# A start-up stage re-ordered: dummies, transposes, weights and first tiles moved in a fused attention and gated feed-forward kernel

## The chip, the cores and the metric

The kernel runs on one core of one Trainium2 chip. The metric is device time in microseconds of one execution; the kernel before was run three times, and its time is the median. A profile is one more execution, recorded by the hardware profiler. The engines are named as in the profile: PE is TensorE's matrix multiply, PEld its weight load, DVE is VectorE, ACT is ScalarE, POOL is GpSimd, SP is SyncE, which issues DMAs only. Each engine works through its own queue in the order in which the program was written, and waits at semaphores for others.

## The reference

Two layers follow each other: an attention with 32 learned inducing points over each batch (`mab` is used twice), and a feed-forward with a sigmoid gate.

```python
def mab(q, kv):                       # m = 32, C = 128, scale = 1/sqrt(C)
    s = scale * (q @ kv.transpose(0, 2, 1))
    s = s - s.max(-1, keepdims=True)
    a = np.exp(s)
    a /= a.sum(-1, keepdims=True) + 1e-09
    return a @ kv
h = mab(I, x)                         # x: (4, 12416, 128), I: (4, 32, 128)
y = mab(x, h)                         # (4, 12416, 128)
gate = 1.0 / (1.0 + np.exp(-(y @ w_gate)))   # w_gate, w_val: (128, 1536)
out = (gate * (y @ w_val)) @ w_out           # w_out: (1536, 128)
```

So there are two stages to each batch. Stage 1 reduces the whole of x to h, 32 rows of 128. Stage 2 gives each token 32 weights on those rows, and the feed-forward follows. The second `a @ kv` is never formed: h is multiplied into w_gate and w_val first (`hw`), so that a token's 32 weights are turned directly into its 1536 gate and value numbers.

## The kernel before

A batch's 12416 tokens are 97 chunks of 128: six groups of 16 (`groups[0]` to `groups[5]`) and one chunk alone (`groups[6]`). The core works on batch 0's stage 1 first. This is the prologue, some 34 us, with nothing else to run beside it; in the loop that follows, stage 1 and the weights of later groups and batches run in slots beside the feed-forward.

**The prologue's stage 1.** x of batch 0 is loaded by groups, in the order of `arrival`: 0, 6, 1, 2, 3, 4, 5. The last group is loaded as 12 chunks and then 4. For each group TensorE transposes the chunks (`x_turn`, line 637), VectorE and ScalarE copy the result to `xT` (639, 641), TensorE computes the scores (`s1_score_pe`, 210), VectorE their maximum, negated (`s1_max`, 222), ScalarE the exponentials (`s1_exp`, 235), TensorE turns these (`s1_turn_pe`, 248), VectorE copies them out (`s1_turn_copy`, 254), and TensorE sums x with them as weights (`s1_sum_pe`, 270). Each group has a maximum of its own. The first four groups to arrive are joined early by GpSimd (`pool_part`, 676 and 680, into `hpart[0]`). The last three, `sa` = 3, `sb` = 4 and `sc` = 5, are joined at the end: `ml` is the least negated maximum of each row (714), L719 and L720 turn `ml` and lay the group maxima `nml` into one tile `low_ps`, VectorE takes the least over the four row groups (`top`, 723), L733 adds it to all rows, and ScalarE's exponential of that is the factor of each group (`wl`, 743). The sums are scaled by `wl` and added by matmuls with e32 (`h_add`, 762); the denominators are summed into `e32l` and through L768 inverted (330). Their product is `hT` (335).

**Last group.** Its first eight chunks go through `x_turn`; the last eight through a tile `xt` of two banks, at line 695. ScalarE copies the first four (697), VectorE the last four (701).

**Dummies.** `keep_on(n, tag)` issues n matmuls of 512 columns on constant data (line 103), whose results nobody reads. Their operand `idle` is the last four chunks of `xT[0]`, which are overwritten only when the last group's last four chunks are copied in; after that a dummy reads those.

**From hT to the loop.** TensorE computes the scores of the first 16 chunks of stage 2 (443), four of them first, and `hw` (341, copied by ScalarE at 351). The first four chunks (block 0) take a short way: maximum, exponential, sum and inverse on VectorE and ScalarE, then sixteen transposes (808) into `a2T`, and two copies by VectorE into `a2first` (812).

**The loop.** A block is four chunks, 512 tokens. Its 12 slices of 128 columns (`j`) are worked on in eight steps of two or one slices. In a step TensorE fills the gate (`g`) and the value (`v`) banks (`hidden_mm`, 853), ScalarE takes the tanh of the gate (873), VectorE forms the product (886), and TensorE projects it through `wo16` into `acc` (917). `hidden_mm` takes rows 0 or 32 of `hw` for a gate and 64 or 96 for a value, by `j % 2`. The gate of step t + 2 is filled behind the value of step t. `blocks[i]` lists the pieces of a block as (batch, first chunk, chunks); before, block 0 has one piece, and only the very first gate fill is cut in two halves, by `cut`.

PSUM tiles with the same tag (g1, v1, g2, v2, m, acc) share their banks: a tile waits until the one before it is read.

## Time and profile before

| | us |
|---|---|
| median of three runs | 726.5 |
| lowest and highest | 725.6 and 726.69 |
| the profiled execution | 728.19 |
| its span | 726.4 |
| first tanh of the loop starts | 33.97 |

The profiled execution is 1.8 us longer than its span, which is what lies around it, and 1.7 us above the median. Rows of the timeline read: start, length, engine, line, operation, out<-in, shape and count, and in brackets the idle time of the engine just before and what ended it. In the chain of waits each row is a piece of the path that ended last: start, length, what. Lengths of a group of several instructions reach from the first's start to the last's end.

### The profile page before, as it was taken

Reading aid. Unit: us, or ns where it says so; the run is one execution under the profiler, and the core shown is the slowest. Engines: PE = TensorE matmul, PEld = TensorE weight load, DVE = VectorE, ACT = ScalarE, POOL = GpSimd, SP = SyncE. Lnnn points to the kernel's source line nnn. Section 1 sums busy time; section 2 is a strip of 40 time slices with the busy share of each in tenths; the row PEclk is TensorE's granted clock in tenths of the full one; section 3 lists DMA queues with packets and bytes.
Section 4 is the critical chain, followed back from the end, with each engine's and each line's share of the span. In section 5 each row is a group of like instructions: output and inputs, shape, how many; then the busy total and the mean of one; then the engine's idle time right before and its main releaser. Section 6 shows DMA issues by size and latency. Waiting matters only on the chain.

```text
span 726.4 us, 21535 instructions
## 1 busy us (share of the span) xinstructions
PE 647.0 (89%) x8461; PEld 391.5 (54%) x8461; DVE 704.7 (97%) x870; ACT 673.9 (93%) x1007; POOL 419.6 (58%) x702
## 2 busy tenths in 40 slices
PE   6888898999998988999988989999999899898887
PEld 3555555555555555555555555555555555555555
DVE  4699999999999999999999999999999999999998
ACT  4499999999999999999999999999999999999996
POOL 4373845788754548488657265387865665636200
PEclk9999999999999999999999999999999999999999
DMA  9789654152649262325177531320322123121211
GB/s 171 133 164 194 130 107 102 59 109 70 83 115 172 69 138 69 80 74 120 51 111 168 104 84 39 80 75 30 76 59 74 45 60 62 53 63 45 61 45 46
DMA packets 116726, 65.21 MB, mean 90 GB/s; under 512 B 99824, under 2 KB 101008, under 8 KB 116624
## 3 DMA queue, kind: packets, MB, share of 16 engines
q1 hardware_dynamic: 111936, 49.81, 30.7%
q0 software_dynamic: 4416, 13.90, 10.7%
q8 instruction: 66, 1.08, 0.7%
q14 instruction: 36, 0.29, 0.2%
q10 hardware_dynamic: 272, 0.13, 0.1%
HBM read 27.80 MB, written 25.43 MB: 73 GB/s over the span
## 4 chain that ended last, share of the span: by engine, by line
DVE 50%; issue 20%; PE 15%; ACT 10%; DMA 3%; DVEq 1%; POOL 0%; SPq 0%; ACTq 0%; POOLq 0%
DVE u L886 48%; ACT t L873 9%; PE acc_ps L917 7%; PE v_ps L853 6%; DMA xn<-in_x_dram 2%; DVE nm L222 1%; DVEq L886 1%; DMA xT<-xn 1%; PE hp_ps L270 1%; PE g_ps L853 1%; PE s_ps L210 0%; POOL xn L81 0%; PE xt_ps L637 0%; ACT a1T L235 0%; ACT hwt L351 0%
## 5 line engine op out<-in xcount | busy, mean ns | idle before, releaser
L886 DVE SCALAR_TENSOR_TENSOR u<-t,v_ps 128x512 f16<-128x512 f16 (+1 forms) x778 | 675.6, 945 | 1.8 <-PE g_ps L853 0.9
L873 ACT ACTIVATE t<-g_ps 128x512 f16<-128x512 f32 (+1 forms) x777 | 594.0, 818 | 28.8 <-ACT t L873 16.9
L853 PE MATMUL v_ps<-a2r,hwt 32*128 32x512 f16 (+1 forms) x1188 | 293.3, 371 | 65.7 <-DVE u L886 65.0
L917 PE MATMUL acc_ps<-wo,u 128*128 128x128 f16 x4656 | 327.4, 220 | 0.0
L917 PEld LDWEIGHTS <-u 128*128 128x128 f16 x4656 | 261.0, 98 | 87.9 <-issue 86.9
L853 PE MATMUL g_ps<-a2r,hwt 32*128 32x512 f16 (+1 forms) x1188 | 296.5, 377 | 0.0
L853 PEld LDWEIGHTS <-hwt 32*128 32x128 f16 x2402 | 90.7, 91 | 197.8 <-issue 152.8
L512 POOL TENSOR_TENSOR sum<-e 128x256 f32<-128x256 f16 (+1 forms) x23 | 15.4, 672 | 144.1 <-ACT e L504 142.6
L558 POOL TENSOR_TENSOR a2n<-e,rs 128x2048 f16<-128x2048 f16 (+3 forms) x25 | 86.8, 3474 | 5.3 <-DVE rs L530 2.4
L536 POOL TENSOR_TENSOR near<-sme,minus 128x16 f32<-128x16 f32 (+1 forms) x22 | 65.2, 2963 | 1.8
L935 ACT ACTIVATE o<-acc_ps 128x512 f32<-128x512 f32 x96 | 58.3, 607 | 0.0
L491 POOL TENSOR_SCALAR rise<-rise 128x256 f32<-128x256 f32 (+6 forms) x110 | 51.0, 464 | 9.7
L490 POOL TENSOR_TENSOR rise<-sc 128x256 f32<-128x256 f32 (+1 forms) x22 | 16.2, 738 | 38.8 <-ACT sc L480 38.5
L492 POOL TENSOR_TENSOR top<-top,rise 128x128 f32<-128x128 f32 (+3 forms) x88 | 28.3, 321 | 7.3
L512 POOL TENSOR_TENSOR sum<-sum 128x128 f32<-128x128 f32 (+3 forms) x92 | 28.3, 307 | 7.2
L490 POOL TENSOR_TENSOR rise<-top 128x128 f32<-128x128 f32 (+3 forms) x88 | 27.2, 309 | 6.9
L495 POOL TENSOR_TENSOR sc<-sc,top 128x512 f32<-128x512 f32 (+1 forms) x22 | 23.8, 1084 | 1.7
L443 PEld LDWEIGHTS <-xT 128*128 128x128 f16 x388 | 13.2, 96 | 11.7 <-issue 11.7
L443 PE MATMUL s_ps<-hT,xT 128*128 128x32 f16 x388 | 18.1, 178 | 0.3 <-DVE hT L335 0.3
L235 ACT ACTIVATE a1T<-s_ps,nm 128x512 f16<-128x512 f32 (+1 forms) x25 | 15.7, 629 | 2.0 <-DVE nm L222 2.0
L492 POOL TENSOR_TENSOR top<-sc,rise 128x256 f32<-128x256 f32 (+1 forms) x22 | 16.3, 739 | 1.8
L81 POOL DMA_DIRECT2D xn<-in_x_dram x25 | 14.7, 597 | 4.4 <-DMA xn<-in_x_dram 3.6
(131 smaller groups left out, 237.0 us busy)
## 6 DMA issues: line engine op xcount, KB each, us to landing
out_dram<-o SPq DMA_DIRECT2D x96, 256.0 KB, 2.3
xn<-in_x_dram POOLq DMA_DIRECT2D x19, 512.0 KB, 8.2
xn<-in_x_dram POOLq DMA_DIRECT2D x4, 544.0 KB, 5.8
a2r<-a2n SPq DMA_TRANSPOSE x29, 4.5
xn<-in_x_dram POOLq DMA_DIRECT2D x1, 384.0 KB, 14.9
wg<-in_moe_w_gate_dram POOLq DMA_DIRECT2D x1, 384.0 KB, 16.3
wv<-in_moe_w_val_dram POOLq DMA_DIRECT2D x1, 384.0 KB, 16.6
wo<-in_moe_w_out_dram POOLq DMA_DIRECT2D x1, 384.0 KB, 16.0
```

The source lines that it names most:

```text
L443: nc.tensor.matmul(s2[:, j, :], xT[b][:, c + j, :], hT16[b][:], start=(j == 0), stop=whole and j == j1 - 1, skip_group_check=True,)
L490: nc.gpsimd.tensor_tensor(out=r, in0=far, in1=near, op=ALU.subtract)
L491: nc.gpsimd.tensor_scalar_max(out=r, in0=r, scalar1=0.0)
L492: nc.gpsimd.tensor_tensor(out=top[:, 0:n, 0:w], in0=near, in1=r, op=ALU.add)
L512: nc.gpsimd.tensor_tensor(out=d[:, 0:n, :], in0=src[:, :, 0:w], in1=src[:, :, w : 2 * w], op=ALU.add)
L536: nc.gpsimd.tensor_tensor(out=near[:, 0:n], in0=sme[:, 0:n], in1=minus1[:, 0:n], op=ALU.pow)
L558: eng.tensor_tensor(out=a2n[:, 0:n, :, :], in0=e.unsqueeze(2).to_broadcast((P, n, 4, m)), in1=rs.unsqueeze(2).unsqueeze(3).to_broadcast((P ...
L853: st[what + "end"] = nc.tensor.matmul(pt[:, k, col : col + nb * P], hw[b][r : r + 32, j // 2, :], a2r[r : r + 32, o : o + nb, :].rearrange ...
L873: st["tanh"] = nc.scalar.activation(out=st["t"][:, :, c:e], in_=st["g"][:, :, c:e], func=AF.Tanh, scale=0.5)
L886: u = nc.vector.scalar_tensor_tensor(out=st["u"][:, :, c:e], in0=st["t"][:, :, c:e], scalar=1.0, in1=st["v"][:, :, c:e], op0=ALU.add, op1= ...
L917: nc.tensor.matmul(acc[0][(i // 2) % len(acc[0])][:, i, :], st["u"][:, k, ts(i, P)], wo16[:, NI * (j % 2) + j // 2, :], start=(j == 0 and ...
L935: nc.scalar.mul(out=o32[:], in_=acc[0][0][:], mul=0.5)
```

## The change

- The five dummies behind the first two groups' transposes are gone.
- The last four transposes of x go to a tile of their own (tag g1), with VectorE's copy right behind them; the two dummies now stand behind that copy in the program.
- The matmul of all group maxima stands ahead of that of `ml`.
- The transposes of sc's weights stand ahead of the four matmuls that add the maximum (now line 726).
- sb's weights are copied by ScalarE. The factor `wl` is applied to `hpart[0]` by GpSimd (was ScalarE) and to sb's sum by ScalarE (was VectorE); the denominators' steps (740, 742, 744) move from GpSimd to VectorE, and `h_add` takes 1, then the denominators, then 0, 2, 3.
- The first weights `a2T` and `a2first` become two tiles of two chunks each, transposed and copied one after the other. Block 0 has two pieces of two chunks, so each of its fills is two matmuls of 256 columns; in step 0's gate the pieces go half by half, elsewhere slice by slice.

On TensorE, around the last transposes. Before (`xt_ps_393` is the last group's tile, `w_ps` the dummies, `s1_ps` the scores):

```order
L103 MATMUL w_ps_403<-xT_0_87 128x512 [waits PE_49]
L103 LDWEIGHTS xT_0_87
L103 MATMUL w_ps_403<-xT_0_87 128x512
L210 LDWEIGHTS indT_146
L210 MATMUL s1_ps_411<-xT_0_87,indT_146 32x512 [waits DVE_49]
```

After, at the same place:

```order
L694 MATMUL xt_ps_392<-ident_116,xn_0_92 128x128
L103 LDWEIGHTS xT_0_87 [waits DVE_49]
L103 MATMUL w_ps_398<-xT_0_87 128x512 [waits Activation_49]
L103 LDWEIGHTS xT_0_87
L103 MATMUL w_ps_398<-xT_0_87 128x512
L210 LDWEIGHTS indT_146
L210 MATMUL s1_ps_405<-xT_0_87,indT_146 32x512 [waits PE_49]
```

The dummies have a new wait for VectorE, which is the copy of the last four chunks; the scores' wait for that copy has moved up to them.

On TensorE, the two matmuls on the maxima. Before:

```order
L248 LDWEIGHTS a1T_350
L248 MATMUL aT_ps_442<-ident_116,a1T_350 128x128
L719 MATMUL low_ps_441<-identf_96,ml_439 1x128 [waits DVE_49]
L720 MATMUL low_ps_441<-nml_134,identf_96 128x4
L248 LDWEIGHTS a1T_407 [waits Activation_49]
L248 MATMUL aT_ps_451<-ident_116,a1T_407 128x128
```

After:

```order
L248 LDWEIGHTS a1T_343
L248 MATMUL aT_ps_435<-ident_116,a1T_343 128x128
L712 MATMUL low_ps_442<-nml_134,identf_96 128x4 [waits DVE_49]
L713 MATMUL low_ps_442<-identf_96,ml_433 1x128 [waits DVE_49]
L248 LDWEIGHTS a1T_401 [waits Activation_49]
L248 MATMUL aT_ps_447<-ident_116,a1T_401 128x128
```

They have changed places, and each has a wait of its own: the first for the last maximum, the second for the minimum that follows it.

On TensorE, the four matmuls that add the maximum (`top_`) and the transposes of sc's weights (`a1T_437` before, `a1T_431` after). Before:

```order
L270 MATMUL hp_ps_460<-xn_0_92,a1_447 32x128
L733 MATMUL low_ps_441<-ones_122,top_456 32x4 [waits DVE_49,Pool_49]
L733 MATMUL low_ps_441<-ones_122,top_456 32x4 x3
L248 LDWEIGHTS a1T_437 [waits Activation_49]
L248 MATMUL aT_ps_481<-ident_116,a1T_437 128x128
```

After:

```order
L248 LDWEIGHTS a1T_431
L248 MATMUL aT_ps_471<-ident_116,a1T_431 128x128
L726 MATMUL low_ps_442<-ones_122,top_445 32x4 [waits DVE_49,Pool_49]
L726 MATMUL low_ps_442<-ones_122,top_445 32x4 x3
L270 LDWEIGHTS a1_452 [waits Activation_49]
L270 MATMUL hp_ps_492<-xn_0_92,a1_452 32x128 [waits PE_49]
```

The transposes are now ahead, and sb's sums, which follow, wait for ScalarE's copy.

The diff, cut to its core:

```diff
@@ -248,10 +248,10 @@
...
-    def s1_turn_copy(s, aT):
+    def s1_turn_copy(s, aT, copy=nc.vector.tensor_copy):
         ng, w, R = s1_dims(s)
         a1 = s1p.tile([P, 4, P], F16, tag="a1")
-        nc.vector.tensor_copy(out=a1[:, 0:w, 0:R], in_=aT[:, 0:w, 0:R])
+        copy(out=a1[:, 0:w, 0:R], in_=aT[:, 0:w, 0:R])
         return a1
...
@@ -646,8 +646,6 @@
...
             x_turn(0, *groups[arrival[p + 2]], ("g2", "v2")[p % 2])
-            if p < 0:
-                keep_on((3, 2)[p + 2], "acc")
         if p + 1 >= 0:
...
@@ -690,16 +688,12 @@
...
     x_turn(0, c0, GC // 2, "g2")
-    xt = ps.tile([P, 2, 8, P], F16, tag="v2", name="xt_ps")
-    for j in range(GC // 2):
-        nc.tensor.transpose(xt[:, j // BC, j % BC, :], xn[0][:, c0 + GC // 2 + j, :], ident[:])
-        if j == BC - 1:
-            two = nc.scalar.copy(
-                out=xT[0][:, c0 + GC // 2 : c0 + n - BC, :], in_=xt[:, 0, 0:BC, :]
-            )
+    for j0, tag, copy in ((GC // 2, "v2", nc.scalar.copy), (GC - BC, "g1", nc.vector.tensor_copy)):
+        xt = ps.tile([P, BC, P], F16, tag=tag, name="xt_ps")
+        for j in range(BC):
+            nc.tensor.transpose(xt[:, j, :], xn[0][:, c0 + j0 + j, :], ident[:])
+        copy(out=xT[0][:, c0 + j0 : c0 + j0 + BC, :], in_=xt[:])
     keep_on(2, "acc")
-    one = nc.vector.tensor_copy(out=xT[0][:, c0 + n - BC : c0 + n, :], in_=xt[:, 1, 0:BC, :])
-    tc.declare_no_dep(one.ins, two.ins, reason="each reads a bank of its own")
     a1T[sb] = s1_exp(0, sb, s1)
...
@@ -712,13 +706,11 @@
...
     nc.vector.tensor_reduce(out=ml[:], in_=nml[:], axis=AX.X, op=ALU.min)
+    a1[sa] = s1_turn_copy(sa, s1_turn_pe(0, sa, a1T[sa]))
     low_ps = ps.tile([P, 2, 512], F32, tag="v2", name="low_ps")
     mlT_ps, arg_ps = low_ps[0:1, 0, 0:P], low_ps[:, 1, 0:NL]
-    aT = s1_turn_pe(0, sa, a1T[sa])
-    a1[sa] = s1_turn_copy(sa, aT)
+    nc.tensor.matmul(arg_ps, identf[:], nml[:], start=True, stop=True, skip_group_check=True)
     nc.tensor.matmul(mlT_ps, ml[:], identf[:], start=True, stop=True)
-    nc.tensor.matmul(arg_ps, identf[:], nml[:], start=True, stop=True, skip_group_check=True)
-    aT = s1_turn_pe(0, sb, a1T[sb], "g2")
     top = const.tile([1, m], F32, tag="top")
...
@@ -727,8 +719,9 @@
...
     )
-    a1[sb] = s1_turn_copy(sb, aT)
+    a1[sb] = s1_turn_copy(sb, s1_turn_pe(0, sb, a1T[sb], "g2"), nc.scalar.copy)
     hps = [s1_sum(0, sa, a1[sa], "acc")]
+    a1[sc] = s1_turn_copy(sc, s1_turn_pe(0, sc, a1T[sc], "v1"))
     for g in range(4):
...
@@ -738,36 +731,35 @@
...
         )
-    aT = s1_turn_pe(0, sc, a1T[sc], "v1")
     wl = const.tile([P, NL], F32, tag="wl")
...
     hw_parts = [hpart[0][:]] + [hst[:, NS - k, 0:C] for k in range(1, NL)]
-    nc.scalar.mul(out=hpart[0][:], in_=hpart[0][:], mul=wl[:, 0:1])
+    nc.gpsimd.tensor_scalar_mul(out=hpart[0][:], in0=hpart[0][:], scalar1=wl[:, 0:1])
     nc.scalar.mul(out=hw_parts[1], in_=hps[0], mul=wl[:, 1:2])
     lw = const.tile([P, NL], F32, tag="lwl")
-    nc.gpsimd.tensor_tensor(out=lw[:], in0=l1l[:], in1=wl[:], op=ALU.mult)
-    add_tree(lw, NL)
+    nc.vector.tensor_mul(out=lw[:], in0=l1l[:], in1=wl[:])
+    lsum = const.tile([P, 1], F32, tag="lsum0")
+    nc.vector.reduce_sum(out=lsum[:], in_=lw[:], axis=AX.X)
     e32l = const.tile([P, m], F32, tag="e32l0")
-    nc.gpsimd.tensor_scalar(
-        out=e32l[:], in0=e32[:], scalar1=lw[:, 0:1], scalar2=TINY, op0=ALU.mult, op1=ALU.add
+    nc.vector.tensor_scalar(
+        out=e32l[:], in0=e32[:], scalar1=lsum[:], scalar2=TINY, op0=ALU.mult, op1=ALU.add
     )
     hps.append(s1_sum(0, sb, a1[sb], "m"))
-    a1[sc] = s1_turn_copy(sc, aT)
-    nc.vector.tensor_scalar_mul(out=hw_parts[2], in0=hps[1], scalar1=wl[:, 2:3])
+    nc.scalar.mul(out=hw_parts[2], in_=hps[1], mul=wl[:, 2:3])
+    hps.append(s1_sum(0, sc, a1[sc], "g1"))
+    nc.vector.tensor_scalar_mul(out=hw_parts[3], in0=hps[2], scalar1=wl[:, 3:4])
...
-    def h_add(k):
-        nc.tensor.matmul(h_ps[:], hw_parts[k], e32[:], start=(k == 0), stop=(k == NL - 1))
-
-    hps.append(s1_sum(0, sc, a1[sc], "g1"))
-    nc.vector.tensor_scalar_mul(out=hw_parts[3], in0=hps[2], scalar1=wl[:, 3:4])
+    def h_add(k, first=False, last=False):
+        nc.tensor.matmul(h_ps[:], hw_parts[k], e32[:], start=first, stop=last)
+
+    h_add(1, first=True)
+    nc.tensor.matmul(l_ps[:], ones[:], e32l[:], start=True, stop=True)
     h_add(0)
-    h_add(1)
-    nc.tensor.matmul(l_ps[:], ones[:], e32l[:], start=True, stop=True)
     h_add(2)
-    h_add(3)
+    h_add(3, last=True)
     h_take(0, h_ps[:], l_inverse(l_ps[:]))
@@ -802,16 +794,18 @@
...
     )
-    a2T = ps.tile([P, BC, P], F16, tag="m", name="a2T_ps")
-    for j in range(BC):
-        for r in range(4):
-            nc.tensor.transpose(a2T[32 * r : 32 * r + 32, j, :], a2n_a[:, j, :], ident[:])
+    for j0, tag in ((0, "m"), (BC // 2, "v2")):
+        a2T = ps.tile([P, BC // 2, P], F16, tag=tag, name="a2T_ps")
+        for j in range(BC // 2):
+            for r in range(4):
+                nc.tensor.transpose(
+                    a2T[32 * r : 32 * r + 32, j, :], a2n_a[:, j0 + j, :], ident[:]
+                )
+        a2first = s2p.tile([P, BC // 2, P], F16, tag=f"a2first{j0}", name="a2first", bufs=1)
+        nc.vector.tensor_copy(out=a2first[:], in_=a2T[:])
+        for j in range(BC // 2):
+            a2[(0, NLO + j0 + j)] = (a2first, j)
     keep_on(1, "g2")
-    a2first = s2p.tile([P, BC, P], F16, tag="a2first", bufs=1)
-    for j in (0, BC // 2):
-        nc.vector.tensor_copy(out=a2first[:, j : j + BC // 2, :], in_=a2T[:, j : j + BC // 2, :])
-    for j in range(BC):
-        a2[(0, NLO + j)] = (a2first, j)
     nb = GC - BC
...
@@ -834,35 +828,37 @@
...
     blocks.append([(b, 0, NLO) for b in range(B)])
+    blocks[0] = [(0, NLO, BC // 2), (0, NLO + BC // 2, BC // 2)]
     for i in range(len(blocks)):
...
-    def hidden_mm(st, what, cut=BC):
+    def hidden_mm(st, what, halves=False):
         pt = ps.tile([P, st["cnt"], 512], F32, tag=f"{what}{st['cnt']}", name=f"{what}_ps")
-        for i in range(0, BC, cut):
-            for k in range(st["cnt"]):
-                j = st["j0"] + k
-                r = 32 * (j % 2 + (2 if what == "v" else 0))
-                col = i * P
-                for b, c, nb in blocks[st["block"]]:
-                    a2r, o = a2[(b, c)]
-                    o, nb = o + i, min(nb, cut)
-                    st[what + "end"] = nc.tensor.matmul(
-                        pt[:, k, col : col + nb * P],
-                        hw[b][r : r + 32, j // 2, :],
-                        a2r[r : r + 32, o : o + nb, :].rearrange("p j t -> p (j t)"),
-                        start=True,
-                        stop=True,
-                    )
-                    col += nb * P
+        pieces, col = [], 0
+        for b, c, nb in blocks[st["block"]]:
+            pieces += [(k, b, c, nb, col) for k in range(st["cnt"])]
+            col += nb * P
+        if not halves:
+            pieces.sort(key=lambda p: p[0])
+        for k, b, c, nb, col in pieces:
+            j = st["j0"] + k
+            r = 32 * (j % 2 + (2 if what == "v" else 0))
+            a2r, o = a2[(b, c)]
+            st[what + "end"] = nc.tensor.matmul(
+                pt[:, k, col : col + nb * P],
+                hw[b][r : r + 32, j // 2, :],
+                a2r[r : r + 32, o : o + nb, :].rearrange("p j t -> p (j t)"),
+                start=True,
+                stop=True,
+            )
         st[what] = pt
...
         if t < NST:
-            hidden_mm(steps[t], "g", BC if t else BC // 2)
+            hidden_mm(steps[t], "g", t == 0)
...
@@ -934,7 +930,7 @@
...
                 b, c, nb = block[0]
-                nc.sync.dma_start(ov[b, :, c : c + nb, :], o32[:])
+                nc.sync.dma_start(ov[b, :, c : c + BC, :], o32[:])
                 if now < NST:
...
```

## The prediction

> **What bounds the kernel now.** I read the busy times of the engines from the loop's start to the end first, then the chain of waits through the prologue, then the timeline at the places that the change touches, and last the granted clock by microsecond. The busy times (stretch, then PE, PEld, DVE, ACT, POOL, clock, DMA):
>
> ```profile
> 34.00:726.40 692.40, 620.53 (x8127) 376.30 (x8124) 687.11 (x816) 658.84 (x974) 406.39 (x667) 1.00 0.40 86
> ```
>
> VectorE (DVE) is busy for 687.11 of the loop's 692.40 us. So the loop is bound by VectorE's products and its length is nearly fixed. All that this change does lies ahead of 34 us or in the loop's first eight steps; a microsecond by which the first product comes sooner should come off the end unchanged. The chain shows which wait ends last in the prologue (start, length, what):
>
> ```profile
> 4.00 14.13 DMA xn<-in_x_dram
> ...
> 22.27 0.43 PE xt_ps L695 x4
> ...
> 24.70 0.39 PE s_ps L210
> ...
> 25.11 0.70 DVE nml L222
> ...
> 25.83 0.17 DVE ml L714
> ...
> 26.05 0.38 PE low_ps L719 x2
> 26.43 0.32 PE low_ps L720 x2
> 26.74 0.24 PE aT_ps L248 x4
> 26.98 0.34 PE hp_ps L270 x16
> 27.32 0.17 PE low_ps L733 x8
> 27.49 0.34 PE aT_ps L248 x4
> ...
> 27.86 0.44 DVE a L254
> ...
> 28.34 0.41 PE hp_ps L270 x16
> ...
> 30.03 0.20 DVE hT L335
> ...
> 33.10 0.30 DVE a2first L812
> ...
> 33.54 0.37 PE g_ps L853 x3
> ...
> 33.97 1.09 ACT t L873 x2
> ```
>
> Until 18.13 us the load of x is the chain; what stands ahead of that on TensorE (PE) waits for data in the end. From there to the first tanh at 33.97 us it is one chain of small dependent steps, and three of the change's parts sit on it.
>
> **The change part by part.** *Five early dummies out.* The rows of both groups, and of the last full group of x that the load brings:
>
> ```profile
> 7.86 0.81 PE L103 MATMUL w_ps<-xT 128*128 128x512 f16 x3
> ...
> 8.72 0.59 PE L103 MATMUL w_ps<-xT 128*128 128x512 f16 x2
> ...
> 18.17 1.07 PE L637 MATMUL xt_ps<-ident,xn 128*128 128x128 f16 x16 [1.96 <-DMA xn<-in_x_dram]
> ```
>
> They end at 9.31, and at 18.17 TensorE has stood idle for 1.96 us, waiting for the load. Removed: 0.00 us, hidden by the load. [...]
>
> *Last four transposes in a tile of their own, dummies after their copy.* The timeline at this place:
>
> ```profile
> 21.96 0.58 PEld L695 LDWEIGHTS <-xn 128*128 128x128 f16 x5
> ```
> ```profile
> 22.31 0.69 DVE L639 COPY xT<-xt_ps 128x1024 f16<-128x1024 f16 x1 [0.26 <-PE xt_ps L637]
> ...
> 22.73 0.58 ACT L697 COPY xT<-xt_ps 128x512 f16<-128x512 f16 x1 [1.13 <-PE xt_ps L695]
> ...
> 23.36 0.38 PE L695 MATMUL xt_ps<-ident,xn 128*128 128x128 f16 x4 [0.67 <-ACT xT L697]
> ...
> 23.58 0.59 PE L103 MATMUL w_ps<-xT 128*128 128x512 f16 x2
> ...
> 24.11 0.40 PE L210 MATMUL s_ps<-xT,indT 128*32 128x512 f16 x3
> 24.22 0.42 DVE L701 COPY xT<-xt_ps 128x512 f16<-128x512 f16 x1 [1.22 <-PE w_ps L103]
> ```
>
> Today the last four transposes wait 0.67 us for ScalarE (ACT) to copy the first four out of the same tile. It is not the data that they wait for: the fifth weight load, which is the first of the last four, had already been issued with the others by 22.54 us. Then the two dummies run, which read the very columns of xT that the copy writes, so VectorE's copy waits for them (1.22 us idle) and the last score starts at 24.70. With the change the last four follow the first four at once: issued to about 22.8, done near 22.95. VectorE's other copy ends at 23.00, so the copy of the last four runs 23.0 to 23.43. The dummies now read what it wrote, so they wait for it: start 23.47. The scores follow the dummies' start by 24.11 - 23.58 = 0.53: 24.00 to 24.40 for all four together, as three took 0.40. The maximum then starts at 24.42 to 24.45 instead of 25.11. Queued behind the waiting dummies are only the scores and what needs them, so the new wait is paid once, in this sum. Gain 0.67 us; bounds: 1.22, VectorE's whole idle time there, and 0.1, if ScalarE's copy, which ends at 23.31, held TensorE after all and the dummies started later than now for the copy behind it.
>
> *Maxima's matmuls swapped, last group's weights ahead of the maximum's broadcast.* Call M the end of the last maximum (25.80 now). Now: minimum over the columns to 26.00, then L719 from 26.05 and L720 to 26.75 = M + 0.95, on which VectorE's `top` waits. After: the matmul of all the maxima needs only M and can issue at M + 0.06; it holds TensorE 0.24 to 0.32 (L720's row), so L719 follows near M + 0.33 instead of M + 0.25, ends 0.38 later at M + 0.71, and `top` waits for that alone. The rest of TensorE's queue by the chain's slots: sb's transposes 0.24, sa's sums 0.34, then directly sc's transposes, without the 0.17 of L733 between. They are issued near M + 1.27 and end at M + 1.67; VectorE's copy of the weights 0.44, the sums start near M + 2.2. Now they start at 28.34 = M + 2.54. Gain 0.34. From below the gain ends at 0.17, the L733 slot alone; from above at 0.17 + 0.32 = 0.49, if L720 vanished from the path too.
>
> *Copy of sb's weights to ScalarE, scalings redistributed.* The rows for their prices:
>
> ```profile
> 25.92 0.60 POOL L676 TENSOR_SCALAR hpart<-hst,we 128x128 f32<-128x128 f32 x1 [3.00 <-ACT hst L285]
> ...
> 27.56 0.17 ACT L743 ACTIVATE wl<-low_ps 128x4 f32<-128x4 f32 x1 [0.89 <-PE low_ps L733]
> ...
> 28.65 0.29 POOL L751 TENSOR_SCALAR e32l<-e,lw 128x32 f32<-128x32 f32 x1
> ```
>
> A copy of 512 columns takes ScalarE 0.58 (L697) where VectorE took 0.44; it runs M + 1.1 to M + 1.7, and sb's sums come up at M + 1.76, so it just fits: 0.00, with 0.1 at risk. The exponential `wl` is behind that copy on ScalarE's queue, but it waits for the broadcast until M + 1.9 anyway. GpSimd (POOL) needs 0.60 for its scaling, to about M + 2.8, and VectorE's three small steps for e32l reach M + 2.75; the five matmuls after sc's sums want them at M + 2.8 (e32l) and M + 3.0 (the scaled part, now third). That fits too: the five stand behind sc's sums in both kernels, so from there to hT at 30.03 nothing changes. 0.00, with at most 0.29 lost (e32l's row) if the small steps slip.
>
> *First weights in two tiles.* The transposes:
>
> ```profile
> 32.64 0.41 PE L808 MATMUL a2T_ps<-ident,a2n_a 128*32 128x128 f16 x16
> ```
>
> The first of VectorE's two copies (33.10) needs only the first eight of these sixteen, which take 0.41 together; of it half the time in which they start is saved, 0.10, so it can start that much sooner, and with it the second copy, the gate fills and the first tanh: the tanh waits for the fills of both halves in both kernels. Gain 0.10, between 0 and 0.20.
>
> *Block 0 in two halves.* All 24 fills of the first block (eight steps, gate and value) become two matmuls of 256 columns each; the two of the very first gate step were cut already. What a fill looks like today, and the loop's first stall:
>
> ```profile
> 38.33 0.39 PE L853 MATMUL v_ps<-a2first,hwt 32*128 32x512 f16 x2
> 38.34 0.39 PE L853 MATMUL g_ps<-a2first,hwt 32*128 32x512 f16 x2
> ```
> ```profile
> 42.99 3.55 DVE L886 SCALAR_TENSOR_TENSOR u<-t,v_ps 128x1024 f16<-128x1024 f16 x4 [0.30 <-PE g_ps L853]
> ```
>
> Four fills of 512 columns run side by side, starting 0.01 apart, since each uses another quarter of the rows. Cut in two and written half after half of one fill, neighbours use the same rows and must follow each other. My estimate: half a fill streams for about 0.11 (a little over a quarter of 0.39, the rest being latency), so a group of four ends 0.3 later and a pair 0.1. Much of it is covered by VectorE's and ScalarE's queues; at 42.99, where VectorE waits for TensorE, I find about 0.15 left after following the slots through the eight steps. Loss 0.15, between 0 and 0.6 (two of the four-fill groups fully exposed).
>
> The sum: 0.67 + 0.34 + 0.10 - 0.15 = 0.96 us less. Against the profiled execution, 728.19 us with a span of 726.4, that is 727.2; the median of the runs shown, 726.5, is 1.7 below the profiled one, so I predict 726.5 - 1.0 = **725.5 us**, 0.13% less. A measurement of this kernel can tell about 0.2%, 1.45 us, from no change, so my likeliest case is a true gain that is called the same.
>
> **The clock.**
>
> ```profile
> 17.00:18.00 1.00, 0.00 (x0) 0.00 (x0) 0.11 (x2) 0.87 (x4) 0.05 (x1) 1.00 1.02 195
> ...
> 19.00:20.00 1.00, 1.00 (x12) 0.46 (x10) 0.72 (x2) 0.72 (x1) 0.92 (x3) 0.57 1.07 211
> ...
> 21.00:22.00 1.00, 1.00 (x12) 0.77 (x9) 0.64 (x1) 0.60 (x3) 0.22 (x1) 0.50 1.09 215
> 22.00:23.00 1.00, 0.69 (x7) 0.54 (x6) 0.74 (x2) 0.27 (x1) 0.83 (x2) 0.72 1.14 187
> ```
>
> The third number from the end is the granted TensorE clock. After almost two microseconds with no matmul it is 0.57, 0.50, 0.72: half speed from about 19.14 to 22.56, 3.4 us, in the middle of the chain. At half speed 3.4 us lose at most 1.7. The idle time that brought it on is the load's and is the same after the change.
>
> [...]
>
> **The rivals.** [...] Chance 0.07.
>
> (2) *The gain is eaten in block 0.* If the four-fill groups of steps 2 to 6 are exposed, 0.6 instead of 0.15, and the ScalarE copy or e32l slips by 0.3, then 726.5 - 0.2 = 726.3: no change. For it: the stall at 42.99 shows TensorE late there today. Against: VectorE's run is unbroken before it. Chance 0.20.
>
> (3) *More than the sum.* The half-speed stretch need not lie at the same place in each run; if in most runs of the changed kernel it misses the chain, up to 1.7 more: 723.8, in the middle 724.6. For it: the runs shown spread by 1.1 us. Against: that would favour the kernel before as well. Chance 0.18.
>
> **How the numbers follow.** Forecast 725.5: 0.55, with its own range of 724.8 to 726.2. The range of 8 in 10 takes in rivals 2 and 3 up to their middle and leaves out a third window: 724.3 to 727.0. Faster by over 0.2% is below 725.05: rival 3's 0.18 and some 0.10 of the forecast's lower side, 0.28. Slower is above 727.95: rival 1, 0.07. The rest, 0.65, is the same.
>
> **What would show it.** Right: no wait of the last transposes for ScalarE; the dummies waiting about 0.5 us for VectorE's copy; the last maximum starting 0.67 sooner against the load's end at 18.13; sc's sums starting M + 2.2; hT about 1.0 and the first tanh about 1.1 sooner; TensorE's groups of four fills 0.3 longer in block 0 and VectorE's stall at its end there or a little larger. Wrong: a clock of 0.5 before 18 us with the chain's start after the load moved; a chain that passes through ScalarE's copy of sb's weights or GpSimd's scaling; VectorE idle by more than 0.6 us in the first eight steps.

## The result, and the profile after

The changed kernel takes 729.29 us (median of seven runs, 728.27 to 731.03); the kernel before, in the same series, 726.5. The ratio is 1.004, with a 95% interval of 1.0023 to 1.0056: slower by 0.4%, where 0.13% faster was forecast. The profiled execution took 729.32 us, with a span of 727.5.

The prologue did get faster. The timeline of the changed kernel, at the places of the prediction's rows:

```profile
16.63 1.07 PE L637 MATMUL xt_ps<-ident,xn 128*128 128x128 f16 x16 [0.64 <-DMA xn<-in_x_dram]
...
19.79 0.61 PE L694 MATMUL xt_ps<-ident,xn 128*128 128x128 f16 x8
...
21.07 0.60 PE L103 MATMUL w_ps<-xT 128*128 128x512 f16 x2 [0.67 <-DVE xT L695]
...
22.06 0.69 DVE L222 TENSOR_REDUCE nml<-s_ps 128x1 f32<-128x512 f32 x1 [0.71 <-PE s_ps L210]
...
23.54 0.28 DVE L715 TENSOR_REDUCE top<-low_ps 1x32 f32<-1x128 f32 x1 [0.26 <-PE low_ps L713]
...
26.95 0.19 DVE L335 TENSOR_TENSOR hT<-h_ps,li 128x32 f16<-128x32 f32 x1 [0.31 <-PE h_ps L756]
...
31.69 4.59 ACT L869 ACTIVATE t<-g_ps 128x512 f16<-128x512 f32 x7 [1.04 <-PE v_ps L850]
```

hT comes at 26.95 instead of 30.03 and the first tanh at 31.69 instead of 33.97, 2.28 us sooner. So more than 3 us went astray behind it. The busy times from VectorE's first product to the end (stretch, length, then PE, PEld, DVE, ACT, POOL, clock, DMA), first of the kernel before, then of the changed one:

```profile
34.60:726.40 691.80, 619.93 (x8123) 376.09 (x8121) 687.05 (x815) 658.24 (x973) 406.13 (x666) 1.00 0.40 86
```
```profile
32.30:727.50 695.20, 622.40 (x8142) 377.64 (x8140) 687.16 (x815) 658.44 (x973) 407.14 (x666) 1.00 0.40 86
```

VectorE has the same work, 687.1 us, and the loop is 3.4 us longer: VectorE's idle time in it (length less busy) rose from 4.75 to 8.04 us. The place is found by cutting the span into stretches of 25 us and then of 1 us. It is one place only (changed kernel, same columns):

```profile
56.00:57.00 1.00, 0.37 (x5) 0.16 (x5) 1.00 (x2) 1.00 (x3) 0.76 (x3) 1.00 0.81 163
57.00:58.00 1.00, 0.00 (x0) 0.00 (x0) 0.65 (x1) 0.65 (x1) 0.83 (x1) 1.00 1.46 57
58.00:59.00 1.00, 0.37 (x4) 0.11 (x3) 0.00 (x0) 0.00 (x0) 0.00 (x0) 0.71 0.90 199
59.00:60.00 1.00, 1.00 (x9) 0.38 (x6) 0.70 (x2) 0.14 (x1) 0.00 (x0) 0.50 0.99 218
...
65.00:66.00 1.00, 1.00 (x17) 0.67 (x14) 0.96 (x2) 0.71 (x2) 0.00 (x0) 0.88 0.64 131
```

TensorE stops at 56.4, starts again at 58.6, and then runs at half clock until 65.24. The timeline there says what it waited for, and who waited for it:

```profile
55.16 0.84 PE L913 MATMUL acc_ps<-wo,u 128*128 128x128 f16 x12
...
58.63 0.62 PE L210 MATMUL s_ps<-xT,indT 128*32 128x512 f16 x4 [2.27 <-DMA xT<-xn]
59.30 0.69 DVE L222 TENSOR_REDUCE nm<-s_ps 128x1 f32<-128x512 f32 x1 [1.65 <-PE s_ps L210]
59.72 1.46 PE L913 MATMUL acc_ps<-wo,u 128*128 128x128 f16 x12
61.78 1.82 DVE L882 SCALAR_TENSOR_TENSOR u<-t,v_ps 128x1024 f16<-128x1024 f16 x2 [1.20 <-PE g_ps L850]
...
64.14 1.82 DVE L882 SCALAR_TENSOR_TENSOR u<-t,v_ps 128x1024 f16<-128x1024 f16 x2 [0.54 <-PE g_ps L850]
```

L210 is the first score of batch 1 (its stage 1 runs in slots of batch 0's loop). It reads the first 16 chunks of x that a DMA transposes into `xT` (line 90, the first entry, 9, of the tuple `(9, 11, 14, 17, 20, 23, 12)` of slots). VectorE loses 1.65 us in the wait and 1.20 + 0.54 us behind it, where a group of twelve projections takes 1.46 instead of 0.84: together 3.39 us, all that the loop lost. The kernel before has the same wait, shorter, and with no half clock behind it:

```profile
59.51 0.40 PE L210 MATMUL s_ps<-xT,indT 128*32 128x512 f16 x4 [0.86 <-DMA xT<-xn]
```

Why the transposition is late is in the view of the DMA queues. The issue is not late: SP issues it at 52.35 us, 2.25 sooner than before (54.60), which is what the prologue gained. From this issue to TensorE's stop at the wait it is 4.0 us in both kernels (58.65 less 54.60, 56.37 less 52.35): the issue moved with the loop. From issue to landing, first in the kernel before (issues between 54.5 and 56 us), then in the changed one (52 to 54 us):

```profile
xT<-xn SPq DMA_TRANSPOSE x1, 4.9
```
```profile
xT<-xn SPq DMA_TRANSPOSE x1, 6.2
```

The stretches 56 to 57 and 57 to 58 us of the changed kernel (the row GB/s has 40 equal slices; a queue's row has packets, MB, share of 16 engines):

```profile
GB/s 205 225 256 215 184 215 184 246 266 266 176 113 134 42 31 20 21 41 41 10 20 10 31 666 51 61 113 143 164 195 215 236 174 236 215 215 246 225 195 205
...
q8 instruction: 1, 0.02, 5.8%
...
GB/s 225 215 256 195 205 184 184 184 154 133 92 72 61 10 41 31 20 0 0 0 0 0 0 0 0 0 0 0 0 0 0 0 0 0 0 0 10 0 0 0
```

A packet of queue q8, instructions, stands in the first stretch, and from 57.4 to 58.3 us the queue of the transpositions (q1) starts hardly a packet. The trace's packet records give the times: the instruction packet has 16 KB, starts at 56.58 and takes 0.93 us. Of the 32 packets of 4 bytes that stand at the end of the transposition in either kernel (completion writes, by their place ahead of the semaphore's increments), 30 have started by 56.60 here; the last two come at 57.50, when the packet is through. The semaphore itself shows more: of the sixteen increments that TensorE waits for, three come by 56.99 and the other thirteen only at 58.30 to 58.59. So more is held back than the two late writes; in what way, the records don't show. In the kernel before the last completion write stands at 58.90 and the sixteen increments at 59.30 to 59.47; the packet comes at 60.35, behind them.

Whose instructions? Call a matmul or a weight load in TensorE's program a row. The changed kernel's page has 66 packets and 1.08 MB on q8; TensorE's program has some 16,900 rows, and 16,900 / 66 is 256 rows for each packet. In the trace TensorE works off 255 rows in the mean from one packet to the next (126 to 357 in single cases). So I take the packets for TensorE's code, one for about 256 rows; when a block is fetched then depends on how many rows TensorE has worked off. The change took 10 rows away ahead of this wait (five dummies, a weight load and a matmul each) and put 44 in (block 0's 24 fills in halves, of which two were cut already: 22 more matmuls with their loads). The wait stands at row 1192 of the program instead of 1158 (the trace counts 39 rows more ahead of it in either kernel, 1231 and 1197, since an f32 matmul stands there in several: L733's four are eight records). The fetch keeps its row instead: in all the fourteen profiles of this document the fifth packet starts when TensorE has begun 1208 to 1251 rows of the trace, while the wait stands anywhere from 1183 to 1295.

### The profile page after: what moved, and what is told of

It is laid out like the page before. It is cut to its first block, busy times and chain, and to the rows that moved or that the text cites. A ratio compares the mean times of both kernels' runs of the same rounds, so it can differ in the third digit from the quotient of the medians.

```text
span 727.5 us, 21568 instructions
## 1 busy us (share of the span) xinstructions
PE 649.0 (89%) x8478; PEld 392.9 (54%) x8478; DVE 704.4 (97%) x871; ACT 674.6 (93%) x1008; POOL 420.4 (58%) x699
## 3 DMA queue, kind: packets, MB, share of 16 engines
q1 hardware_dynamic: 111936, 49.81, 31.1%
q8 instruction: 66, 1.08, 0.6%
## 4 chain that ended last, share of the span: by engine, by line
DVE 50%; issue 21%; PE 16%; ACT 9%; DMA 3%; DVEq 1%; POOL 0%; ACTq 0%; POOLq 0%
DVE u L882 48%; ACT t L869 8%; PE acc_ps L913 7%; PE v_ps L850 6%; DMA xn<-in_x_dram 2%; DVE nm L222 2%; DMA xT<-xn 1%; DVEq L882 1%; PE hp_ps L270 1%; PE g_ps L850 1%; POOL xn L81 0%; PE w_ps L103 0%; PE s_ps L443 0%; ACT hwt L351 0%; PE s_ps L210 0%
## 5 line engine op out<-in xcount | busy, mean ns | idle before, releaser
L222 DVE TENSOR_REDUCE nm<-s_ps 128x1 f32<-128x512 f32 (+1 forms) x25 | 15.5, 618 | 2.3 <-PE s_ps L210 2.3
## 6 DMA issues: line engine op xcount, KB each, us to landing
wo<-in_moe_w_out_dram POOLq DMA_DIRECT2D x1, 384.0 KB, 16.1
```

## The experiments

Three theories. F: the fetch, moved by 34 rows, falls into the transposition on which TensorE waits. E: the loop, 2.3 us sooner, comes to the transposed input too early whatever the fetch does. B: block 0 in halves costs the loop. In the table, "fetch" is the packet of q8 nearest to the wait, "offset" its start less the time at which TensorE stops at the wait, "landing" the time from issue to landing of batch 1's first transposition, "wait" that of L210, "idle" VectorE's from its first product to the end, in the profiled execution; "median" is of all runs. The kernels stand by their row: with more rows ahead the fetch comes sooner against the wait, from some 3 us behind it to 3 us ahead, and from row 1192 on it is inside the transfer. With the transposition left in its slot, the five transfers with a fetch inside take 5.7 to 6.5 us to land, the five without 4.6 to 4.9.

```
kernel             row of wait  fetch   offset  issue  landing   wait   idle   median
e4_after_whole         1144     58.7     +3.1   51.54    4.8     0.78   4.75   725.42
e9_before_no_five      1148     59.4     +3.0   52.35    4.8     0.77   4.70   725.77
e8_whole_five          1154     61.6     +3.2   54.39    4.8     0.78   4.77   725.9
before                 1158     60.3     +1.7   54.60    4.9     0.86   4.75   726.5
e12_before_again       1158     57.9     +1.1   52.74    4.6     0.53   4.57   726.45
changed                1192     56.6     +0.2   52.35    6.2     2.27   8.04   729.29
e7_whole_plus48        1192     57.2     +0.4   52.71    6.5     2.45   7.11   729.93
e3_after_five          1202     55.7     -1.2   53.02    5.7     1.81   7.53   728.5
e2_before_plus48       1206     59.3     -1.1   55.96    6.2     1.91   9.01   729.38
e1_after_plus64        1256     54.8     -3.1   53.79    5.7     1.63   7.39   728.65
e5_after_slot7         1192     54.7            42.28   11.2     none   4.68   724.72
```

**Rows moved, array work unmoved.** In the kernel before, dummies of 512 columns were cut in four matmuls of 128 columns each; nothing else was touched:

```diff
-    def keep_on(n, tag):
+    def keep_on(n, tag, quarters=0):
...
-        for _ in range(n):
-            nc.tensor.matmul(w_ps[:], idle[:, 0, :], idle, start=True, stop=True)
+        for k in range(n):
+            if k < quarters:
+                for q in range(4):
+                    nc.tensor.matmul(w_ps[:, q, :], idle[:, 0, :], idle[:, q, :], start=True, stop=True)
+            else:
+                nc.tensor.matmul(w_ps[:], idle[:, 0, :], idle, start=True, stop=True)
...
-    keep_on(8, "acc")
+    keep_on(8, "acc", 3)
...
-                keep_on((3, 2)[p + 2], "acc")
+                keep_on((3, 2)[p + 2], "acc", 3)
```

> The kernel before with 48 more rows on TensorE ahead of the loop and the same array work (the five early dummies, and three of the eight, cut in four matmuls of 128 columns each). Theory F: the fetch now falls into the first transposition of sample 1 as it does in the changed kernel; TensorE's wait there grows from 0.86 us to 1.8 or more, half clock follows, 728.5 to 731 us although nothing else is changed. Theories E and B: no change, 726.5.

Measured: 729.38 us, ratio 1.004 (1.0025 to 1.0054). Forty-eight rows of dummies slow the kernel before by as much as the whole change did. Its wait, in the timeline:

```profile
62.24 0.40 PE L216 MATMUL s_ps<-xT,indT 128*32 128x512 f16 x4 [1.91 <-DMA xT<-xn]
```

This execution also had half clock from 29.9 to 43.6 us, which is part of its 9.01 us idle. Theories E and B forecast no change and fall as the whole cause.

The changed kernel with 64 rows more, by the same helper (`quarters`), the five early dummies back in quarters:

```diff
+            if p < 0:
+                keep_on((3, 2)[p + 2], "acc", 3)
...
-    keep_on(8, "acc")
+    keep_on(8, "acc", 4)
```

> The changed kernel with 64 more rows on TensorE ahead of the loop and the same array work: the five early dummies are back as twenty matmuls of 128 columns, and four of the eight after inducing's transposition are cut in four. Theory F (TensorE's own instruction fetch, a packet of 16 KB that takes 0.93 us, falls into the first DMA transposition of sample 1 in the changed kernel, holds one ring's share of it and so makes TensorE wait 2.27 us, after which the half clock comes): 64 rows earlier it comes some 4 us sooner in the loop and misses that transposition; the wait is back at 0.7 to 1.0 us, no half clock behind it, and what the prologue gained (the first tanh at 31.7 instead of 34.0) is kept: 724.2 us, 723.8 to 725.2. Theory E (the loop simply reaches sample 1's transposed input too early, whatever the fetch does): as the changed kernel, 729.3. Theory B (block 0 in halves costs it): 729.3.

Measured: 728.65 us, 1.0032 (1.0018 to 1.0046). F's number, 724.2, missed. The fetch did move as forecast, 3.3 us against TensorE's stop, to 54.8 us; but the transposition had been issued at 53.79, 4.1 us ahead of the stop, and was hit all the same, earlier in its transfer: the last 32 of its completion writes all came late (58.61 to 58.91), not two of them. So a fetch 1.0 us behind the issue hit the transfer here, not only one in its last microseconds. Nor is it "one ring's share" that is seen to be held: no record shows rings, and thirteen of the sixteen increments were late in the changed kernel.

**Block 0 whole.** The changed kernel without the cut, which is 48 rows fewer:

```diff
-    blocks[0] = [(0, NLO, BC // 2), (0, NLO + BC // 2, BC // 2)]
...
+    a2first = s2p.tile([P, BC, P], F16, tag="a2first", name="a2first", bufs=1)
     for j0, tag in ((0, "m"), (BC // 2, "v2")):
...
-        a2first = s2p.tile([P, BC // 2, P], F16, tag=f"a2first{j0}", name="a2first", bufs=1)
-        nc.vector.tensor_copy(out=a2first[:], in_=a2T[:])
+        nc.vector.tensor_copy(out=a2first[:, j0 : j0 + BC // 2, :], in_=a2T[:])
...
-            a2[(0, NLO + j0 + j)] = (a2first, j)
+            a2[(0, NLO + j0 + j)] = (a2first, j0 + j)
```

> The changed kernel with block 0 filled whole, 512 columns a matmul, both copies going into one tile: 48 rows fewer ahead of the wait. Theory F: the fetch comes behind the wait as in the kernel before, wait 0.7 to 1.0 us, no half clock there; the first product waits for both copies, some 0.3 us later: 724.5 us, 723.8 to 725.5. Theory B: the same. Theory E: 729.

Measured: 725.42 us, 0.9989 (0.9976 to 1.0003): the loss is gone, the wait is back at 0.78 us and the fetch behind it. This alone doesn't tell F from B. The next one does: the same kernel with 48 rows put back elsewhere.

```diff
-    keep_on(8, "acc")
+    keep_on(8, "acc", 8)
```

> Block 0 whole, with 48 rows more on TensorE ahead of the loop (the eight dummies behind inducing's transposition cut in four each), which puts the wait at the same row, 1192, as in the changed kernel. Theory F: the fetch falls into the transposition again, 728 to 730 us, VectorE's idle time from its first product on 7 us or more. Theory B: as with block 0 whole, 725.4.

Measured: 729.93 us, 1.0049 (1.0032 to 1.0066). With block 0 whole and the wait at row 1192 again the loss is back. B falls.

```profile
59.22 0.40 PE L216 MATMUL s_ps<-xT,indT 128*32 128x512 f16 x4 [2.45 <-DMA xT<-xn]
```

**The transposition moved, the rows left.** The changed kernel, with batch 1's first transposition in slot 7:

```diff
-            when = 3 * g if b else (9, 11, 14, 17, 20, 23, 12)[g]
+            when = 3 * g if b else (7, 11, 14, 17, 20, 23, 12)[g]
```

> The changed kernel with the first DMA transposition of sample 1 issued two slots sooner (slot 7 instead of 9), so that it has landed some 5 us before TensorE comes to it; the rows of TensorE and with them the fetches stay where they were. Theory F (the fetch inside that transposition): the wait of 2.27 us and the two windows of half clock behind it go, VectorE's idle time from its first product on falls from 7.9 us to about 4.5: 725.4 us, 724.8 to 726. Theory B (block 0 in halves costs the loop): 729.3, for block 0 is still in halves. Theory E (the loop comes too early for the transposed input): the same as F.

Measured: 724.72 us (724.52 to 727.87, ten runs), ratio 0.9978 (0.9963 to 0.9992). It beats both kernels, and by a little more than F forecast. SP issues the transposition at 42.28; it takes 11.2 us there, and has landed at 53.45, 2 us ahead of TensorE's first score (55.40) and not the 5 that were expected. The loop's row and the first tanh:

```profile
31.40:722.80 691.40, 619.69 (x8142) 376.04 (x8140) 686.72 (x815) 658.42 (x973) 407.12 (x666) 1.00 0.40 86
...
30.80 4.59 ACT L869 ACTIVATE t<-g_ps 128x512 f16<-128x512 f32 x7 [0.75 <-PE g_ps L850]
```

VectorE is idle for 4.68 us of the loop, with block 0 still in halves. The fetch of 54.7 comes behind the landing; an earlier one, at 45.9, does fall into the transfer, but nobody waits for it then. Together, the row count moved with the transposition left (e2, e7, e4) and the transposition moved with the row count left (e5) show the cause: the fetch must meet this transfer, and the transfer must be waited for. The same with block 0 whole (both diffs above):

> The same sooner transposition with block 0 whole. The wait of 0.8 us that was left goes too, of which VectorE felt 0.14 us: 725.2 us, 724.7 to 725.8; and fewer slow executions, since no idle time is left there that could bring the half clock.

Measured: 725.33 us, 0.9983 (0.9973 to 0.9993), slowest run 726.17. Its loop has 4.59 us idle against 4.68: the halves cost the loop nothing that can be seen, 0.1 us at the most in these two.

**The five early dummies.** Back in the changed kernel, and back in the one with block 0 whole:

```diff
+            if p < 0:
+                keep_on((3, 2)[p + 2], "acc")
```

> The changed kernel with the five early dummies put back whole, as they stood before: 10 rows more, so the fetch comes about half a microsecond sooner in the loop, still inside the transposition's transfer. Theory F: still slow, 728 to 731. Theory D (the dummies' absence lets the clock fall later): 724 to 726.5. Theory E and B: 729.3.

Measured: 728.5 us, 1.0031 (1.0012 to 1.0049), as F had it.

> Block 0 whole and the five early dummies put back. The loop is left alone (the fetch stays behind the wait). What the dummies themselves cost: nothing, 725.4 us, if they only fill idle time as the prediction had it. If their 10 rows put the first fetch of the prologue back to 16.1 us, into the arrival of the sixth group of the load, that group's transpositions start at 18.2 instead of 16.7 and hT comes at 28.4 instead of 26.9: up to 1.3 us more, 726 to 726.7.

Measured: 725.9 us, 1.0001 (0.9991 to 1.0012), 0.5 above the 725.42 without them, between the two forecasts and with intervals that overlap. And out of the kernel before, alone:

```diff
-            if p < 0:
-                keep_on((3, 2)[p + 2], "acc")
```

> The kernel before with the five early dummies out and nothing else. The prediction's first step priced this at nothing: 726.3 us. If their ten rows decide whether the first fetch of the prologue comes into the arrival of the sixth group: the fetch moves from 16.1 to about 16.5 us, that group's transpositions start at 16.7 instead of 17.8 to 18.2, and the fetch in the loop stays behind the wait (row 1148): 725.2 us, 724.8 to 725.8.

Measured: 725.77 us, 0.9987 (0.997 to 1.0005), beside 726.42 of the kernel before: in the direction of the second reading, but the interval holds no change. The profiles are clearer. First with the five dummies (e8), then without (e9):

```profile
17.94 1.07 PE L637 MATMUL xt_ps<-ident,xn 128*128 128x128 f16 x16 [1.85 <-DMA xn<-in_x_dram]
```
```profile
16.82 1.07 PE L637 MATMUL xt_ps<-ident,xn 128*128 128x128 f16 x16 [0.57 <-DMA xn<-in_x_dram]
```

This is the last full group of the load, the sixth to arrive. TensorE's first fetch of the prologue comes just then. In the packet records of the first profile of the kernel before, fifteen of this group's sixteen completion writes stand at 15.82 to 16.44 us and the last, behind the fetch of 16.1 us, at 17.08; in the changed kernel all sixteen stand at 15.68 to 16.21 and the fetch at 16.5. Over the fourteen profiled executions, the seven with a fetch at 16.3 us or sooner started these transposes at 17.83 to 18.34, and the seven with a fetch at 16.4 or later at 16.63 to 16.82. In the seven early ones the last of the group's sixteen semaphore increments comes 0.9 to 1.6 us behind the fifteenth, in the other seven 0.3 us at most. With the dummies (or more rows) the fetch stood at 15.8 to 16.4, without them at 16.3 to 16.8. So ten rows shift the odds; they don't settle each execution.

**A second profile of the kernel before**, unchanged:

> The kernel before unchanged, for a second profile, since the one shown had half clock from 19.1 to 22.6 us. Without it: 725.5 us, hT at some 28.5 us, the first product about 32.0, the loop from there 691.7 us long.

Measured: 726.45 us (725.94 to 726.87), not the 725.5 that was expected; half clock came at 27.69 to 31.1, and the first product only at 32.77. The fetch stood at 16.4 and missed the group:

```profile
16.80 1.07 PE L637 MATMUL xt_ps<-ident,xn 128*128 128x128 f16 x16 [0.57 <-DMA xn<-in_x_dram]
...
22.56 0.69 DVE L222 TENSOR_REDUCE nml<-s_ps 128x1 f32<-128x512 f32 x1
...
24.23 0.28 DVE L723 TENSOR_REDUCE top<-low_ps 1x32 f32<-1x128 f32 x1 [0.45 <-PE low_ps L720]
...
27.48 0.19 DVE L335 TENSOR_TENSOR hT<-h_ps,li 128x32 f16<-128x32 f32 x1
```

hT at 27.48, without half clock ahead of it: of the 3.08 us by which hT came sooner in the first pair of profiles, 2.55 lay between two executions of the kernel before, and only 0.53 is the change's. These rows, beside the changed kernel's, price the prediction's steps below.

**The other parts.** The kernel before, without the five dummies and with slot 7 (both diffs above), none of the rest:

> The kernel before with the five early dummies out and sample 1's first transposition two slots sooner, none of the change's other parts. Beside the changed kernel with the sooner transposition (724.7 us) it prices the other parts together (the last four transpositions, the order of the maximum's matmuls, the two tiles, the halves): by the prediction 0.9 us, so 725.6; if only the fetches counted, 724.7.

Measured: 725.48 us, 0.9988 (0.9974 to 1.0002). Against e5's 724.72, the rest of the change is worth some 0.8 us where no fetch is in the way (0.6 between the fastest runs, 725.09 and 724.52). Of that, the last four transposes, put back into the shared tile in e5's kernel:

```diff
-    for j0, tag, copy in ((GC // 2, "v2", nc.scalar.copy), (GC - BC, "g1", nc.vector.tensor_copy)):
-        xt = ps.tile([P, BC, P], F16, tag=tag, name="xt_ps")
...
+    xt = ps.tile([P, 2, 8, P], F16, tag="v2", name="xt_ps")
+    for j in range(GC // 2):
+        nc.tensor.transpose(xt[:, j // BC, j % BC, :], xn[0][:, c0 + GC // 2 + j, :], ident[:])
...
     keep_on(2, "acc")
+    one = nc.vector.tensor_copy(out=xT[0][:, c0 + n - BC : c0 + n, :], in_=xt[:, 1, 0:BC, :])
```

> The changed kernel with the sooner transposition, its last four transpositions back in the tile shared with the four before them, their copy behind the two dummies, as in the kernel before. By the prediction's step (b) it loses 0.67 us: 725.4, and hT comes at 27.6 instead of 26.95; if another wait ends there as late, 724.7.

Measured: 725.89 us (724.9 to 730.16), 0.9984 (0.9971 to 0.9998). Its fastest run is 0.38 above e5's fastest, its median 1.17 above. The profiled execution had a fetch at 16.3, which held the load, so hT (28.98) has to be counted from the last group's first transposes (20.83): 8.15 us, against 7.66 in e5 (26.96 less 19.30). The shared tile costs 0.49 us there.

## Why the prediction was wrong

*"A microsecond by which the first product comes sooner should come off the end unchanged."* This step failed, and with it the sign: the first product came 2.3 us sooner, and the end 1.1 us later in the profiles. The loop's own length is as fixed as it was said to be: 691.3 to 691.8 us from the first product in the profiles in which nothing met the transposition and the clock stayed up. But one transfer in it is waited for, and the prediction looked at the loop's busy times only, not at the one DMA wait in it, which the profile of before shows with 0.86 us.

*Block 0 in two halves: "Loss 0.15, between 0 and 0.6".* As a matter of TensorE's time this was too much: halves on the same rows do start 0.11 to 0.12 us apart (`v_ps` at 36.06 and 36.18 us in the changed kernel), but such a group of four takes 0.41 us from its first start to its last end against 0.39 whole, the stall at the block's end is 0.30 us as before (at 40.72), and e5 and e6 differ by 0.1 us at the most in the loop. What was left out is that 22 more matmuls are 44 more rows. They cost 3.4 us, 1.65 in the wait and 1.74 behind it, where the clock was at half, through a queue that the prediction did not count.

*Five early dummies: "Removed: 0.00 us, hidden by the load".* The cover was named, but the load's end isn't independent of TensorE: their ten rows shift a fetch that, when it comes early, holds one of the load's groups by 1.0 to 1.7 us. That is a gain where it happens, and at the end not told apart from nothing (0.9987, 0.997 to 1.0005).

*"The idle time that brought it on is the load's and is the same after the change."* Wrong for the same reason: 1.96 us became 0.64 (and 0.57 in the second profile of the kernel before), and the half clock at 19 us did not come in the changed kernel. It came at 27.69 to 31.11 in the profiled execution, which held the first tanh back to 31.69; in e5, without it, 30.80.

*Last four transposes, 0.67.* Right in mechanism: no wait for ScalarE, the dummies wait 0.67 us for VectorE's copy, the four scores together take 0.40. The last maximum starts at 22.06 against 22.56: 0.50, and e11 shows 0.49. The size was taken from a profile at half clock: there the dummies began 0.58 us behind VectorE's other copy, in the second profile 0.34.

*Maxima's matmuls and sc's weights, 0.34; redistribution, 0.00 with at most 0.29 lost.* `top` starts 1.48 us behind the maximum's start, against 1.67, and sc's sums start 2.27 us behind the maximum's end, against 2.54: 0.27 gained. But from there to hT, where nothing was to change, it takes 1.93 us against 1.69, so hT comes 4.89 behind the maximum's start against 4.92, and 0.03 is left. VectorE's three small steps run to 25.73 us, TensorE's l_ps starts at 25.87, between two of the four h parts, and hT waits 0.31 for the last of these. So 0.24 of the 0.29 that the redistribution could lose at most was lost.

*First weights in two tiles, 0.10.* From hT to the first tanh it takes 3.84 us in e5 against 3.93 in e9, both at full clock: 0.09.

The steps so measured give 0.50 + 0.03 + 0.09 = 0.62 us against 0.96. That would have been 725.9 without the fetch, and e5 and e10 bear it out from the other side (0.8, or 0.6 by the fastest runs).

Of the rivals none was it. With the dummies gone no half clock came ahead of the load's end: no dummy runs between 6.7 and 21.07 us in the changed kernel, and the clock is granted in full from 7.2 to 27.69. The range, which "leaves out a third window: 724.3 to 727.0", counts on such windows in the prologue; no run shows one that the missing dummies brought, and what the change did bring was the half clock from 58.41 to 65.24 us. So the slower side was on the list with the wrong place: half clock did cost, 1.74 us, but behind a wait in the loop.

## What to carry to other kernels

Adding or removing instructions on TensorE, dummies too, moved the fetches of its program here: against the wait the fifth came 0.9 to 1.5 us sooner with 34 rows more (+1.1 and +1.7 to +0.2) and 2.2 to 2.8 us sooner with 48 (to -1.1). So count rows as well as microseconds, and look in the trace for transfers that are waited for and lie within a few microseconds of a packet of the instruction queue. Such a transfer is best issued earlier: two slots for one DMA transposition turned a loss of 0.4% into a gain of 0.2%. And two profiles of the kernel before are worth having: a gain read from one pair was four fifths the difference between two executions of the same kernel.

## What the runs showed of the hardware

At the transposition one instruction packet of 16 KB, 0.93 to 1.02 us long, went with a landing of the 512 KB some 0.8 to 1.9 us later (5.7 to 6.5 us from issue to landing against 4.6 to 4.9). It held back more than one part of it: 18 to 21 packets of 256 bytes of the transpositions then under way, whose median is 0.02 us, took 0.8 to 1.6 us, and in the changed kernel thirteen of sixteen increments of the semaphore were late. In the kernel before the packet at 60.35 went with 20 such packets of the next transposition (1.28 to 1.60 us), and no engine waited for that one. Not every long packet goes with a fetch: fifteen of 0.56 to 0.94 us stand at 53.28 to 53.66 us in the kernel before, and fifteen of 0.61 to 0.76 us at 51.10 to 51.27 in the changed one, with no packet of q8 near. The plain load of the sixth group had one late increment of sixteen, 0.9 to 1.6 us behind the others; in the kernel before this goes with one completion write of sixteen behind the packet (17.08 us, the increment at 18.13). Why thirteen are late for the transposition and one for the load, the records don't show.

TensorE stood idle for 1.5 to 2.5 us twelve times in the first 75 us of the fourteen profiles. Eight of these times half clock came, from 0.5 us ahead of their end to 1.8 us behind it, among them all five at the transposition; four times (1.48 to 2.12 us, all waits for the load) it didn't. The nine profiles without a long wait at the transposition had none at that place. But six more stretches of half clock, beginning at 27.7 to 30.9 us, had no idle time over 1.2 us in the 9 us ahead of them; what brought these on stays open. Half clock came in stretches of 3.41 us or several times that (58.41 to 65.24 is two, 29.9 to 43.6 in e2 and 30.94 to 44.59 in e11 are four). Why it lasted for four in e2 and e11 stays open: TensorE was busy for 13.54 of the 13.6 us in e2.
